# Building the first group's x parts in place, and k^T v head by head, in a one-core attention plus two-MLP kernel

## The chip, the cores and the metric

The kernel runs on one core of a Trainium2 chip. The metric is device time of one execution in microseconds (us), lower is better. The times of the kernel before are three executions; the profile is of a separate, fourth one.

## What is computed

Linear attention for 4 batches and 8 heads, 576 tokens of 64 features: per head `kv = k^T v` (64 x 64), `out = q kv`, then a root-mean-square norm of each token's 64 features with a gain. The heads are put side by side to 2304 tokens of 512 features, and two MLPs follow, each `x -> act(x w_in) w_out` with 2048 hidden features; the first act is softplus, the second a leaky ReLU of slope 0.01. All in float32:

```python
kv = einsum('bhsd,bhse->bhde', k, v);  out = einsum('bhsd,bhde->bhse', q, kv)
x = out / sqrt(mean(out * out) + 1e-06) * g_norm      # then heads side by side
x = softplus(x @ w_in) @ w_out                        # moe_
x = leaky_relu(x @ w_in, 0.01) @ w_out                # moe2_
```

The weights arrive as 64-bit floats; "decode" below makes float32 of them.

## The kernel before, in words

**Order of the work.** Every piece of work is registered with `op(cost, fn, reads, writes)`; `Plan.run` is a list scheduler that goes through all of them at build time with estimated costs (PE, A = ScalarE, D = VectorE, P = GpSimd, S = a DMA issued by SyncE, N = nothing) and due times, and so fixes the order of instructions on each engine. In the times it assumes, DMAs of kind S share one DMA resource; the reload of x parts that GpSimd issues (line 784) stands in it as 1.0 us of GpSimd time.

**Attention.** A unit is two heads of one batch, 16 units in all. `load(u)` brings q, k, v (five units ahead at most). `T(u)` copies q and k from the loaded order (partition, head, row, feature) to (partition, row, head, feature) in `qp` and `kp` (lines 337 to 341, on whichever engine the plan picks), transposes q on TensorE (lines 397, 401) and makes k^T v of both heads at once (lines 405, 408): four 128 x 128 matmuls and one over the 64 left-over tokens. The 128 x 128 result holds the two wanted 64 x 64 blocks on its diagonal; line 423 multiplies it by a block mask of ones and zeros into `kvm`. `O(u)` multiplies q by `kvm` (lines 436, 442), `normal` makes the norm, `X(u)` transposes the normed tokens into `xy` (features x tokens).

**MLPs.** Tokens are taken in 3 tiles of 768 (2 blocks of 384), hidden features in groups of 512 (4 groups for each MLP). In every group and tile there are two steps s, each with seven products of a Strassen-like scheme in float32r with hi and lo parts: `product(s, i)` (line 802, six matmuls) reads weights from `wst` and the x part `xe[i]`; `after` makes the activation; `quarter` multiplies by w_out (lines 900 and 916) one step later. The seven x parts of a tile are sums or differences of 384-token blocks of `xy`: `minus` (line 740) where a difference is needed, then `split_part`: a ScalarE copy to float32r (line 711) and a subtraction for the low part (line 706). There is one set of seven buffers `xe`, so a part of the next tile can go into `xe[i]` only after the second step's `product(s, i)` has read it.

**x parts in the first group of each MLP.** The first tile's parts are made in `xe` itself during attention. For tiles 1 and 2 the four parts that are differences (1, 2, 4, 6) are made one step ahead in a two-buffer stage `rc`, stored to the DRAM scratch `xscr` (line 758) and then brought into `xe[i]` by a GpSimd-issued DMA (line 784) once `xe[i]` is free; the three plain parts (0, 3, 5) are split straight from `xy` into `xe[i]`. In the later groups all parts come from `xscr`.

**Buffers.** `mf` (24 KiB for each partition) and `lf` (7 KiB, free only once attention's norm is done) hold among others two raw weight buffers `raw` (both in `mf`, used in turn by the weight chunks), the decoded weights `sraw`/`half`, and the activation inputs `cA` (one in `mf`, one in `lf`) and `cB`.

Of the kernel before, what the change touches and what calls it, by code (L numbers as in the profile page):

```python
# [8 lines left out]
F32 = mybir.dt.float32  # L9
F32R = mybir.dt.float32r  # L10
I32 = mybir.dt.int32
# [8 lines left out]
class Plan:  # L20
# [9 lines left out]
    DMA_ISSUE, DMA_START, DMA_DONE = 0.57, 1.1, 1.0  # L30

# [31 lines left out]
    def span(self, o):  # L63
        if "S" in o["cost"]:
            return self.DMA_ISSUE + self.DMA_START + o["cost"]["S"] + self.DMA_DONE
        return min(o["cost"].values())

    def run(self):
# [3 lines left out]
        free = {e: 0.0 for e in ("PE", "A", "D", "P", "S", "N")}  # L72
# [16 lines left out]
        while True:  # L89
            best = None  # L90
            for e, c in cand.items():
                if not c:
                    continue
                t = max(free[e], min(o["at"][e] for o in c))
# [16 lines left out]
            if e == "S":  # L111
                free[e] = t + self.DMA_ISSUE
# [16 lines left out]
def linear_attention_two_mlps(  # L129
# [36 lines left out]
    P = 128  # L166
# [37 lines left out]
    mask = const.tile([P, P], F32, name="mask")  # L204
    nc.vector.memset(mask, 0.0)
    nc.vector.memset(mask[0:D, 0:D], 1.0)
    nc.vector.memset(mask[D:P, D:P], 1.0)
# [13 lines left out]
    SIZE = {"ra": 70, "mf": 24, "rb": 54, "rc": 12, "lf": 7}  # L221
# [43 lines left out]
    raw = [Reg("mf", at * KI, [DM, 2], I32) for at in (0, 4)]  # L265

    SRAW = (("mf", 8), ("lf", 0))
# [11 lines left out]
    xt = [Reg("mf", at * KI, [2, BN]) for at in (12, 15)]  # L279
# [5 lines left out]
    cB = Reg("mf", 21 * KI, [2, BN])  # L285
    cA = [Reg("mf", 18 * KI, [2, BN]), Reg("lf", 4 * KI, [2, BN])]
# [15 lines left out]
    kp = ring(attp, "kp", 2, [P, 4, 2, D])  # L302
# [9 lines left out]
    fm = ring(mstp, "fm", 2, [P, 20])  # L312
    for t_ in ss:
        nc.vector.memset(t_, 1.0)
# [65 lines left out]
    def T(u):  # L380
# [3 lines left out]
        for nm, dst in (("q", qp), ("k", kp)):  # L384
            copy_to(
                dst[i], lda[nm][u % NLD].rearrange("p h r d -> p r h d"), 512,
                [(nm, u % NLD)], [(nm + "p", i)],
            )
        p0 = 2 * i if u < U_H else 0
        p1 = p0 + 1  # L390
        kv = ps[p1][:, 2 * P:3 * P]
# [11 lines left out]
        def f_kv(e):  # L403
            for r in range(4):
                nc.tensor.matmul(  # L405
                    kv, kp[i][:, r, :, :], va[:, :, r, :], start=(r == 0), stop=False
                )
            nc.tensor.matmul(kv, kl[:, h2, :], vl[:, h2, :], start=False, stop=True)  # L408

        for j in range(2):  # L410
# [6 lines left out]
            if j:  # L417
                op(
                    {"PE": 1.1}, f_kv,
                    [("kp", i), ("v", u % NLD), ("kr", b % 2), ("vr", b % 2)], [("ps", p1)],  # L420
                )
                op(
                    {"D": 0.22}, lambda e: nc.vector.tensor_tensor(kvm[i], kv, mask, ALU.mult),
                    [], [("ps", p1), ("kvm", i)],
                )
# [129 lines left out]
    def decode_w(F, which, a_reg):  # L555
        ph, f = F // NF, F % NF
        src = ((w1, w2), (w3, w4))[ph][which]
        ri = chunk_no[0] % 2
        chunk_no[0] += 1
        r_, t_ = raw[ri].ap, sqr  # L560
        low, high = r_[:, :, 0], r_[:, :, 1]

        def f_l(e):
            if which == 0:
# [4 lines left out]
            else:  # L569
# [4 lines left out]
        rk, tk, ak = raw[ri].keys(), [("sqr",)], a_reg.keys()  # L574
# [4 lines left out]
                a_reg.ap.bitcast(F32), high.bitcast(F32), AF.Copy, scale=2.0 ** -112  # L579
# [11 lines left out]
                t_, low, 29, t_, ALU.logical_shift_right, ALU.bitwise_or  # L591
# [175 lines left out]
    def x_load(tp, i, at_hand):  # L767
# [3 lines left out]
        if i in PLAIN:  # L771
# [11 lines left out]
            {"P": 1.0},  # L783
# [187 lines left out]
    for i in range(NU + XL):  # L971
# [19 lines left out]
       + [(t, i) for t in ("qp", "kp", "kvm") for i in range(2)]  # L991
# [15 lines left out]
    for s in range(2 * NT2 + 2):  # L1007
# [7 lines left out]
        for i in range(7):  # L1015
            if t < NT2:
                product(s, i)
                after(s, i)
                if t + 1 < NT2 and u == 0 and t + 1 in fresh:
                    x_part((t + 1) % NTP, i, xstage)  # L1020
                if t + 1 < NT2 and u == 1:
                    x_load((t + 1) % NTP, i, t + 1 in fresh)
# [59 lines left out]
```

## Time and profile before

| what | value |
|---|---|
| median of 3 runs | 856.74 us (854.68 to 857.86) |
| profiled execution's own time | 858.63 us |
| its span, first to last instruction | 856.9 us |
| TensorE busy | 830.3 us (97% of the span) |
| VectorE, ScalarE, GpSimd busy | 572.2, 449.5, 97.6 us |
| mean granted TensorE clock | 0.998 of full speed |
| moved by DMA | 172.73 MB |

Busy times of different engines overlap. What lies outside the span is 858.63 - 856.9 = 1.7 us.

### The profile page before, as it was taken

Reading aid. Unit: us, or ns where it says so; the run is one execution under the profiler, and the core shown is the slowest. Engines: PE = TensorE matmul, PEld = TensorE weight load, DVE = VectorE, ACT = ScalarE, POOL = GpSimd, SP = SyncE. Lnnn points to the kernel's source line nnn. Section 1 sums busy time; section 2 is a strip of 40 time slices with the busy share of each in tenths; the row PEclk is TensorE's granted clock in tenths of the full one; section 3 lists DMA queues with packets and bytes.
Section 4 is the critical chain, followed back from the end, with each engine's and each line's share of the span. In section 5 each row is a group of like instructions: output and inputs, shape, how many; then the busy total and the mean of one; then the engine's idle time right before and its main releaser. Section 6 shows DMA issues by size and latency. Waiting matters only on the chain.

```text
span 856.9 us, 11971 instructions
## 1 busy us (share of the span) xinstructions
PE 830.3 (97%) x4512; PEld 772.8 (90%) x4512; DVE 572.2 (67%) x911; ACT 449.5 (52%) x730; POOL 97.6 (11%) x152
## 2 busy tenths in 40 slices
PE   7998879999999999999999999999999999999997
PEld 5877769999999999999999998898988889898986
DVE  2779958786558673877778875766568855854332
ACT  1567847666445553645456665755455544553340
POOL 1476210000000000000000000000000000100000
PEclk9999999999999999999999999999999999999999
DMA  9984679667527646547757867645635852643613
GB/s 280 319 260 173 202 283 342 228 209 229 188 88 235 202 142 225 170 153 229 244 198 236 310 242 269 223 165 190 227 95 181 275 172 82 203 147 93 203 49 98
DMA packets 80024, 172.73 MB, mean 202 GB/s; under 512 B 11616, under 2 KB 54112, under 8 KB 79968
## 3 DMA queue, kind: packets, MB, share of 16 engines
q1 hardware_dynamic: 66720, 99.63, 35.0%
q0 software_dynamic: 13248, 72.36, 25.4%
q8 instruction: 35, 0.57, 0.3%
q14 instruction: 21, 0.17, 0.1%
HBM read 141.30 MB, written 30.67 MB: 201 GB/s over the span
## 4 chain that ended last, share of the span: by engine, by line
PE 88%; DMA 5%; DVE 4%; ACT 2%; issue 1%; POOL 0%; SPq 0%; POOLq 0%; DVEq 0%
PE ps L802 38%; PE ps L900 22%; PE ps L916 22%; PE ps L436 2%; DMA ra<-xscr 1%; DMA mf<-in_moe_w_in_dram 1%; PE ps L405 1%; DMA xscr<-rc 1%; PE ps L397 1%; PE ps L528 1%; DMA qa<-in_q_dram 1%; PE ps L442 1%; PE ps L408 1%; DVE xn L506 0%; DVE ra L659 0%
## 5 line engine op out<-in xcount | busy, mean ns | idle before, releaser
L802 PE MATMUL ps<-ra 128*128 128x384 f32 x2016 | 406.0, 336 | 10.0 <-DMA ra<-xscr 7.7
L802 PEld LDWEIGHTS ps<-ra 128*128 128x128 f32 x2016 | 357.4, 188 | 27.0 <-issue 6.5
L900 PE MATMUL ps<-rb 128*128 128x384 f32 x1152 | 227.1, 335 | 0.0
L916 PE MATMUL ps<-rb 128*128 128x512 f32 x864 | 225.0, 394 | 0.4 <-ACT xy L678 0.4
L900 PEld LDWEIGHTS ps<-rb 128*128 128x128 f32 x1152 | 202.6, 188 | 0.0
L916 PEld LDWEIGHTS ps<-rb 128*128 128x128 f32 x864 | 159.7, 188 | 24.7 <-ACT xy L678 1.1
L832 DVE TENSOR_TENSOR mf<-ps,mf 128x384 f32<-128x384 f32 x120 | 66.7, 557 | 156.5 <-PE ps L802 124.5
L784 POOL DMA_DIRECT2D ra<-xscr x92 | 49.2, 535 | 653.4 <-PE ps L802 605.5
L825 ACT ACTIVATE mf<-ps 128x384 f32<-128x384 f32 x120 | 58.7, 492 | 99.2 <-PE ps L802 98.5
L683 DVE TENSOR_TENSOR xy<-ps,xy 128x384 f32<-128x384 f32 (+1 forms) x126 | 77.4, 614 | 30.1 <-PE ps L916 20.8
L858 DVE TENSOR_TENSOR rb<-mf,rb 128x768 fp32r<-128x768 f32 x72 | 68.4, 951 | 1.9 <-ACT rb L853 1.8
L711 ACT ACTIVATE ra<-mf 128x768 fp32r<-128x768 f32 x58 | 48.7, 841 | 29.8 <-PE ps L802 28.6
L853 ACT ACTIVATE rb<-mf 128x768 fp32r<-128x768 f32 x72 | 61.0, 847 | 2.1
L706 DVE TENSOR_TENSOR ra<-mf,ra 128x768 fp32r<-128x768 f32 x55 | 53.5, 972 | 12.3 <-ACT ra L711 12.0
L845 ACT ACTIVATE mf<-mf 128x768 f32<-128x768 f32 (+1 forms) x36 | 26.6, 739 | 60.1 <-DVE mf L832 60.1
L839 ACT ACTIVATE mf<-mf 128x768 f32<-128x768 f32 (+1 forms) x36 | 26.5, 735 | 45.5 <-DVE mf L832 45.5
L590 DVE SCALAR_TENSOR_TENSOR sqr<-mf,sqr 128x512 int32<-128x512 int32 x64 | 46.9, 733 | 1.2
L578 ACT ACTIVATE mf<-mf 128x512 f32<-128x512 f32 x34 | 22.6, 666 | 27.4 <-DMA mf<-in_moe_w_in_dram 19.8
L678 ACT ACTIVATE xy<-ps 128x384 f32<-128x384 f32 (+1 forms) x33 | 17.4, 531 | 18.0 <-PE ps L900 14.7
L858 DVE TENSOR_TENSOR rb<-lf,rb 128x768 fp32r<-128x768 f32 x24 | 22.9, 954 | 3.7 <-ACT rb L853 3.7
L832 DVE TENSOR_TENSOR lf<-ps,lf 128x384 f32<-128x384 f32 x24 | 13.4, 558 | 16.9 <-PE ps L802 16.8
L596 DVE SCALAR_TENSOR_TENSOR mf<-mf,sqr 128x512 int32<-128x512 int32 x34 | 23.7, 698 | 0.4
(97 smaller groups left out, 646.5 us busy)
## 6 DMA issues: line engine op xcount, KB each, us to landing
ra<-xscr POOLq DMA_DIRECT2D x92, 768.0 KB, 6.0
mf<-xscr SPq DMA_DIRECT2D x54, 384.0 KB, 5.5
mf<-in_moe_w_in_dram SPq DMA_DIRECT2D x32, 512.0 KB, 4.4
mf<-in_moe_w_out_dram SPq DMA_DIRECT2D x32, 512.0 KB, 4.0
xscr<-rc SPq DMA_DIRECT2D x20, 768.0 KB, 4.0
xscr<-xy SPq DMA_DIRECT2D x18, 384.0 KB, 4.8
qa<-in_q_dram SPq DMA_DIRECT2D x16, 256.0 KB, 5.2
ka<-in_k_dram SPq DMA_DIRECT2D x16, 256.0 KB, 5.1
```

Source lines behind the costliest of these rows:

```text
L590: lambda e: nc.vector.scalar_tensor_tensor(t_, low, 29, t_, ALU.logical_shift_right, ALU.bitwise_or), rk + tk, tk,
L683: {"D": t_d(n)}, lambda e: nc.vector.tensor_tensor(dst, src, dst, ALU.add),
L706: ENG[e].tensor_tensor(e_[:, 1, :, :], src(), e_[:, 0, :, :].bitcast(F32), ALU.subtract)
L711: {"A": t_a(n)}, lambda e: nc.scalar.activation(e_[:, 0, :, :], src(), AF.Copy),
L784: lambda e: nc.gpsimd.dma_start(out=flat(xe[i]).ap, in_=xscr[7 * tp + i]),
L802: nc.tensor.matmul(o, w_[:, a, c:c + P], e_[:, b, kk, :], start=(not on and kk == 0 and n == 0), stop=(kk == 1 and n == 2), skip_group_che ...
L825: {"A": t_a(BN)}, lambda e: nc.scalar.activation(c[:, m, :], src, AF.Copy),
L832: lambda e: nc.vector.tensor_tensor(c[:, m, :], src, c[:, m, :], ALU.add),
L853: {"A": t_a(n)}, lambda e: nc.scalar.activation(g[:, 0, :, :], c.ap, AF.Copy),
L858: lambda e: nc.vector.tensor_tensor(g[:, 1, :, :], c.ap, g[:, 0, :, :].bitcast(F32), ALU.subtract),
L900: nc.tensor.matmul(y[:, :BN], w_[m][:, a, js], G_[:, b, m, :], start=(u == 0 and m == 0 and i == 0), stop=(u == 1 and m == 1 and i == 2),)
L916: nc.tensor.matmul(y, G_[:, a, m, js], w_[m][:, b, :], start=(u == 0 and m == 0 and i == 0), stop=(u == 1 and m == 1 and i == 2),)
```

## The change

It does five things. (1) For tiles 1 and 2 of the first MLP's first group, all seven x parts are made in `xe[i]` itself, in the second step, after `product(s, i)` has read the old part; the stage `rc` and the reload from DRAM are left out there, the store to `xscr` for the later groups stays, and the subtractions may also go to GpSimd. The first group of the second MLP keeps the stage. (2) k^T v is made head by head from `ka` as loaded: twice four matmuls with 128 x 64 weights and one over the left-over tokens, the second head into partitions 64 to 127; the copy `kp` is gone. (3) The mask is gone: `kvm` is zeroed once, and two copies of 64 x 64 a unit put the blocks in. (4) The second raw weight buffer moves to `lf`, so the first six weight chunks use one raw buffer; the second `cA` moves to `mf`; `mf` shrinks and `lf` grows by 1 KiB. (5) The plan has a new kind G, a DMA that GpSimd issues, with 2.25 us on the shared DMA resource; the reload of line 784 is now of that kind.

```diff
-        if "S" in o["cost"]:
-            return self.DMA_ISSUE + self.DMA_START + o["cost"]["S"] + self.DMA_DONE
+        if self.DMA_BY.keys() & o["cost"].keys():
+            return self.DMA_ISSUE + self.DMA_START + sum(o["cost"].values()) + self.DMA_DONE
...
-    SIZE = {"ra": 70, "mf": 24, "rb": 54, "rc": 12, "lf": 7}
+    SIZE = {"ra": 70, "mf": 23, "rb": 54, "rc": 12, "lf": 8}
...
-    raw = [Reg("mf", at * KI, [DM, 2], I32) for at in (0, 4)]
+    raw = [Reg(n, at * KI, [DM, 2], I32) for n, at in (("mf", 0), ("lf", 4))]
...
-    cA = [Reg("mf", 18 * KI, [2, BN]), Reg("lf", 4 * KI, [2, BN])]
+    cA = [Reg("mf", at * KI, [2, BN]) for at in (17, 4)]
...
-        for nm, dst in (("q", qp), ("k", kp)):
+        for nm, dst in (("q", qp),):
...
-        kv = ps[p1][:, 2 * P:3 * P]
+        kv = ps[p1][:, 2 * P:2 * P + D]
+        ka = lda["k"][u % NLD]
...
         def f_kv(e):
-            for r in range(4):
+            for h in range(2):
+                o = kv[h * D:(h + 1) * D, :]
+                for r in range(4):
+                    nc.tensor.matmul(
+                        o, ka[:, h, r, :], va[:, h, r, :], start=(r == 0), stop=False
+                    )
                 nc.tensor.matmul(
-                    kv, kp[i][:, r, :, :], va[:, :, r, :], start=(r == 0), stop=False
-                )
-            nc.tensor.matmul(kv, kl[:, h2, :], vl[:, h2, :], start=False, stop=True)
+                    o, kl[:, 2 * hp + h, :], vl[:, 2 * hp + h, :], start=False, stop=True
+                )
...
-                op(
-                    {"D": 0.22}, lambda e: nc.vector.tensor_tensor(kvm[i], kv, mask, ALU.mult),
-                    [], [("ps", p1), ("kvm", i)],
-                )
+                def f_m(e):
+                    for h in range(2):
+                        hs = slice(h * D, (h + 1) * D)
+                        nc.vector.tensor_copy(kvm[i][hs, hs], kv[hs, :])
+
+                op({"D": 0.3}, f_m, [], [("ps", p1), ("kvm", i)])
...
-        ri = chunk_no[0] % 2
+        ri = chunk_no[0] % 2 if chunk_no[0] >= 6 else 0
...
         op(
-            {"P": 1.0},
+            {"G": 2.25},
             lambda e: nc.gpsimd.dma_start(out=flat(xe[i]).ap, in_=xscr[7 * tp + i]),
...
-                if t + 1 < NT2 and u == 0 and t + 1 in fresh:
-                    x_part((t + 1) % NTP, i, xstage)
-                if t + 1 < NT2 and u == 1:
+                straight = t + 1 <= 2
+                if t + 1 in fresh and (not straight and u == 0 or straight and u == 1):
+                    x_part((t + 1) % NTP, i, () if straight else xstage)
+                elif t + 1 < NT2 and u == 1:
                     x_load((t + 1) % NTP, i, t + 1 in fresh)
```

## Rows read from the trace of the kernel before

**Rows 1.** Busy time by stretch: length, each engine (instructions), clock, DMA share, GB/s.
```profile
20.50:57.00 36.50, 36.19 (x251) 29.35 (x251) 27.08 (x61) 21.93 (x47) 19.35 (x28) 1.00 1.04 323
57.00:93.00 36.00, 31.69 (x215) 26.06 (x213) 34.22 (x62) 26.83 (x56) 23.54 (x23) 1.00 0.49 173
93.00:113.00 20.00, 15.16 (x75) 13.53 (x75) 18.87 (x25) 15.83 (x26) 4.83 (x4) 0.91 0.71 251
113.00:124.00 11.00, 7.59 (x42) 7.33 (x43) 2.31 (x4) 2.13 (x4) 1.09 (x2) 1.00 0.87 318
124.00:155.00 31.00, 29.36 (x168) 28.75 (x167) 24.34 (x37) 20.55 (x37) 2.11 (x4) 1.00 0.84 302
155.00:490.00 335.00, 335.00 (x1935) 334.96 (x1934) 241.83 (x382) 185.63 (x290) 22.70 (x43) 1.00 0.61 202
490.00:850.00 360.00, 359.28 (x1776) 320.88 (x1774) 216.73 (x324) 173.08 (x269) 22.08 (x41) 1.00 0.53 174
```

**Rows 2.** What TensorE waited for in the whole span: total us, times, longest.
```profile
PE ps L802 <- DMA ra<-xscr: 7.7, 4, 2.4
...
PE ps L802 <- ACT lf L825: 1.4, 1, 1.4
```

**Rows 3.** Chain of work, 100 to 126 us: start us, us, what.
```profile
106.29 9.87 DMA xscr<-rc
...
116.70 5.54 DMA ra<-xscr
...
123.69 1.05 PE ps L900 x6
124.73 1.04 PE ps L802 x6
```

**Rows 4.** TensorE's timeline, 94 to 128 us: start us, us, instruction, idle before.
```profile
94.28 1.34 PE L802 MATMUL ps<-ra 128*128 128x384 f32 x6
...
109.31 2.13 PE L802 MATMUL ps<-ra 128*128 128x384 f32 x6 [2.44 <-DMA ra<-xscr]
111.24 1.16 PE L900 MATMUL ps<-rb 128*128 128x384 f32 x3
...
126.65 1.20 PE L802 MATMUL ps<-ra 128*128 128x384 f32 x6
```

**Rows 5.** Groups of instructions up to 130 us, by form: count, busy us, mean ns.
```profile
L341 POOL TENSOR_SCALAR kp<-ka 128x512 f32<-128x512 f32 x9 | 5.9, 656 | 7.6 <-issue 2.9 <-PE ps L405 2.6 <-DMA ka<-in_k_dram 2.1
...
L711 ACT ACTIVATE rc<-mf 128x768 fp32r<-128x768 f32 x6 | 5.0, 834 | 0.0
L706 DVE TENSOR_TENSOR rc<-mf,rc 128x768 fp32r<-128x768 f32 x5 | 4.8, 952 | 0.7 <-ACT rc L711 0.7
...
L423 DVE TENSOR_TENSOR kvm<-ps,mask 128x128 f32<-128x128 f32 x16 | 4.6, 286 | 10.8 <-PE ps L408 10.5 <-PE ps L442 0.3
...
L355 DVE COPY qt<-ps 128x256 f32<-128x256 f32 x7 | 2.9, 415 | 0.0
```

**Rows 6.** Chain of work in attention, all on TensorE: start us, us, what.
```profile
9.16 2.00 PE ps L405 x8
...
45.37 0.26 PE ps L540 x2
...
47.11 0.36 PE ps L442 x2
...
50.08 0.20 PE ps L401
...
51.09 0.89 PE ps L405 x8
51.98 0.41 PE ps L408 x2
```

**Rows 7.** DMA issues on the page: count, KB each, median us to landing.
```profile
mf<-in_moe_w_out_dram SPq DMA_DIRECT2D x32, 512.0 KB, 4.0
```

**Rows 8.** TensorE's instructions of line 405 from 20.5 to 57 us, by form.
```profile
L405 PE MATMUL ps<-va,kp 128*128 128x128 f32 x72 | 9.9, 281 | 0.0
```

More of the change, by code (lines that the diff above doesn't have):

```diff
@@ L30 @@
     DMA_ISSUE, DMA_START, DMA_DONE = 0.57, 1.1, 1.0
+    DMA_BY = {"S": "S", "G": "P"}
     def __init__(self):
@@ L71, in run @@
                 o["due"] = min(o["due"], s["due"] - self.LAT - self.span(o))
-        free = {e: 0.0 for e in ("PE", "A", "D", "P", "S", "N")}
+        free = {e: 0.0 for e in ("PE", "A", "D", "P", "S", "G", "N")}
         dma = 0.0
@@ L93, in run @@
                     continue
-                t = max(free[e], min(o["at"][e] for o in c))
+                t = max(free[self.DMA_BY.get(e, e)], min(o["at"][e] for o in c))
                 o = min(
@@ L110, in run @@
             o["eng"], o["start"] = e, t
-            if e == "S":
-                free[e] = t + self.DMA_ISSUE
+            if e in self.DMA_BY:
+                free[self.DMA_BY[e]] = t + self.DMA_ISSUE
                 dma = max(dma, t + self.DMA_ISSUE + self.DMA_START) + o["cost"][e]
@@ L203, in linear_attention_two_mlps @@
     make_identity(nc, ident)
[L204 to L207, printed above, removed]
     graw = const.tile([P, 1], F32, name="graw")
@@ L264, in linear_attention_two_mlps @@
     sqr = const.tile([P, DM], I32, name="sqr")
-    raw = [Reg("mf", at * KI, [DM, 2], I32) for at in (0, 4)]
-    SRAW = (("mf", 8), ("lf", 0))
+    raw = [Reg(n, at * KI, [DM, 2], I32) for n, at in (("mf", 0), ("lf", 4))]
+    SRAW = (("mf", 7), ("lf", 0))
     sraw = [Reg(n, at * KI, [4, 256]) for n, at in SRAW]
@@ L278, in linear_attention_two_mlps @@
     xe = [Reg("ra", 6 * i * KI, [2, 2, BN]) for i in range(7)]
-    xt = [Reg("mf", at * KI, [2, BN]) for at in (12, 15)]
+    xt = [Reg("mf", at * KI, [2, BN]) for at in (11, 14)]
     xstage = [Reg("rc", at * KI, [2, 2, BN]) for at in (0, 6)]
@@ L284, in linear_attention_two_mlps @@
     gA = [Reg("rb", (12 + 6 * i) * KI, [2, 2, BN]) for i in range(3)]
-    cB = Reg("mf", 21 * KI, [2, BN])
-    cA = [Reg("mf", 18 * KI, [2, BN]), Reg("lf", 4 * KI, [2, BN])]
+    cB = Reg("mf", 20 * KI, [2, BN])
+    cA = [Reg("mf", at * KI, [2, BN]) for at in (17, 4)]
     dram = ctx.enter_context(tc.tile_pool(name="dram", bufs=1, space=bass.MemoryType.DRAM))
@@ L301, in linear_attention_two_mlps @@
     qp = ring(attp, "qp", 2, [P, 4, 2, D])
-    kp = ring(attp, "kp", 2, [P, 4, 2, D])
     qt = ring(attp, "qt", 2, [P, S])
@@ L312, in linear_attention_two_mlps @@
     fm = ring(mstp, "fm", 2, [P, 20])
+    for t_ in kvm:
+        nc.vector.memset(t_, 0.0)
     for t_ in ss:
@@ L419, in T @@
                     {"PE": 1.1}, f_kv,
-                    [("kp", i), ("v", u % NLD), ("kr", b % 2), ("vr", b % 2)], [("ps", p1)],
+                    [("k", u % NLD), ("v", u % NLD), ("kr", b % 2), ("vr", b % 2)], [("ps", p1)],
                 )
-                op(
-                    {"D": 0.22}, lambda e: nc.vector.tensor_tensor(kvm[i], kv, mask, ALU.mult),
-                    [], [("ps", p1), ("kvm", i)],
-                )
+                def f_m(e):
[3 more added lines that the diff above has]
+                op({"D": 0.3}, f_m, [], [("ps", p1), ("kvm", i)])
             from_psum(qt[i][:, c0:c0 + n], ps[p0 + j][:, :n], n, p0 + j, [("qt", i, j)])
@@ L557, in decode_w @@
         src = ((w1, w2), (w3, w4))[ph][which]
-        ri = chunk_no[0] % 2
+        ri = chunk_no[0] % 2 if chunk_no[0] >= 6 else 0
         chunk_no[0] += 1
-        r_, t_ = raw[ri].ap, sqr
-        low, high = r_[:, :, 0], r_[:, :, 1]
+        r, t_ = raw[ri], sqr
         def f_l(e):
+            r_ = r.ap
             if which == 0:
@@ L572, in f_l @@
                 )
-        rk, tk, ak = raw[ri].keys(), [("sqr",)], a_reg.keys()
+        rk, tk, ak = r.keys(), [("sqr",)], a_reg.keys()
         op({"S": 1.46}, f_l, (), rk)
@@ L578, in decode_w @@
             lambda e: nc.scalar.activation(
-                a_reg.ap.bitcast(F32), high.bitcast(F32), AF.Copy, scale=2.0 ** -112
+                a_reg.ap.bitcast(F32), r[:, :, 1].bitcast(F32), AF.Copy, scale=2.0 ** -112
             ), rk, ak,
@@ L590, in decode_w @@
             lambda e: nc.vector.scalar_tensor_tensor(
-                t_, low, 29, t_, ALU.logical_shift_right, ALU.bitwise_or
+                t_, r[:, :, 0], 29, t_, ALU.logical_shift_right, ALU.bitwise_or
             ), rk + tk, tk,
@@ L990, in linear_attention_two_mlps @@
     op({"N": 0.0}, attention_done, (), granules("rb")
-       + [(t, i) for t in ("qp", "kp", "kvm") for i in range(2)]
+       + [(t, i) for t in ("qp", "kvm") for i in range(2)]
        + [("qt", i, j) for i in range(2) for j in range(2)]
```

## Prediction

> **What bounds the kernel now.** I first read busy time by stretch. From 155 us TensorE is never short of work: 335.00 of 335 us, then 359.28 of 360 [rows 1]. The change leaves the matmuls there as they are, so it can only win or lose before 155 us, where there are four different stretches. From 20.5 to 57 us TensorE is the bound (36.19 of 36.5 us busy) and VectorE has 9.4 us to spare. From 57 to 93 us VectorE is the bound (34.22 of 36), TensorE idle for 4.3 us. From 93 to 113 us VectorE is still nearly full (18.87 of 20), TensorE idle for 4.84 us. From 113 to 124 us both idle, TensorE 3.41 and VectorE 8.69 us, while the DMA engines are 87% busy; from 124 to 155 TensorE idles for 1.64 us more [rows 1]. Then the waits: `product` (line 802) waited 7.7 us in four waits for x parts coming back from DRAM, and once 1.4 us for ScalarE [rows 2]. The chain says what made them late: the store of a staged part took 9.87 us, its reload 5.54 us [rows 3]. The timeline shows a second price: after the 2.44 us wait, six matmuls take 1.93 us (109.31 to 111.24) instead of the 1.04 us of a warm six [rows 3, 4], in a stretch whose mean granted clock is 0.91 [rows 1].
>
> **The x parts in place: what it can give.** TensorE's idle time from 93 to 155 us is 4.84 + 3.41 + 1.64 = 9.9 us [rows 1]. The slow clock adds 1.93 - 1.04 = 0.9 us for the six matmuls at 109.31 and, for the three at 111.24 (1.16 us of pipelined duration; warm six start to start take 1.05, so three about 0.52), about 0.6 us [rows 3, 4]. Together 11.4 us; this is the ceiling.
>
> What remains of it? In place there is no DMA between product(1, i) and product(2, i), but a chain: ScalarE copy 0.83 us, VectorE subtraction 0.95 us [rows 5], both allowed only once TensorE has read the old part. Seven parts need 7 x 0.83 = 5.8 us of ScalarE and, with four differences of the same length, 11 x 0.95 = 10.5 us of VectorE. That work isn't new: 93 to 113 us holds most of it already, for the stage. VectorE was through its backlog at 113 us. On TensorE, from 94.28 us on, the second step's seven products and the next step's seven are 14 x 1.04 = 14.6 us, and between them lie 16 groups of three w_out matmuls at 0.52 = 8.4 us [rows 3, 4]: 23 us of work, to 117.3 us if nothing stalls, where the last product of these now starts at 126.65 and ends near 127.7 us [rows 4]. Since parts are due one after another and the w_out groups can be put between, a finish of the parts at 108 to 113 us (VectorE's backlog, less what GpSimd takes) fits with little waiting. I allow 2 us of new waits and 1 us of the old ones at the end of attention (table load, last norm), so the gain is 11.4 - 3 = 8.4 us. Bounds: 11 us with no wait, 3 us if VectorE and ScalarE become the gate (rival 2). For tile 2 the parts have a whole step of 15 us and more, with VectorE at 24.34 of 31 us [rows 1], so I charge nothing; if that cover is gone, it costs the 1.64 us counted above.
>
> **k^T v head by head: what it costs.** All rows here are warm and on the chain. Eight matmul records with 128 columns take 0.89 us, 0.111 each; a unit's two with 64 rows take 0.41 us [rows 6], so 0.41 - 2 x 0.111 = 0.19 us goes with the change of the array's shape. Two with 64-wide weights take 0.36 us: 0.14 us for that change. One transpose of 64 columns takes 0.20, two 0.26: 0.06 us for one more record of 64 columns [rows 6]. A unit is now 0.89 + 0.41 = 1.30 us of TensorE. After, it has 20 records of 64 columns and four changes of shape (into 128 x 64, into 64 x 64, for each head): 20 x 0.06 + 2 x (0.14 + 0.19) = 1.86 us, so +0.56 us. The way back to full size is paid in both versions. Bounds: if a 64-column record is no shorter than a 128-column one, 20 x 0.111 + 0.66 = 2.88 us, +1.6 us a unit; if the changes between the heads' halves cost nothing and records follow at half of 0.111, 1.1 us, -0.2 us a unit. I take the middle, since the two transposes are the only records with 64 moving columns.
>
> A rule of the Trainium skill speaks for the upper bound: "TensorE: Matmul & The Clock Gate", Part 3, says that a weight load overlaps running matmuls only where its row group differs, and here all loads of a head have one row group. By it each record pays its load as well as its stream, which gives the upper bound's order of cost. The trace doesn't bear it out for the 128-wide case: loads with one row group lie between the eight records that follow each other every 0.111 us [rows 6].
>
> Where does +0.56 us fall? Nine units run in the TensorE-bound stretch (72 records of line 405 in it, eight a unit [rows 8]): 5.0 us. Two run before, in the first 20 us, where the same eight take 2.00 us instead of 0.89 [rows 6]; at twice the cost they add 2.2 us. The last five run where VectorE is the bound and TensorE's 4.3 us idle covers their 2.8 us; without the cover they are a loss. So TensorE leaves its stretch 7.2 us later. Not all of this reaches 93 us: VectorE, the bound after it, gets 7 us more of spare time ahead of its own stretch and can do part of its backlog (decode, x parts of tile 0) there. I take half, 3.6 us; bounds 0 and 7.2, and for the upper price of a record (9 x 1.6 + 2 x 3.2 = 20.8 us) some 10 to 21 us.
>
> **The rest.** The 16 copies to `kp` vanish; nine were GpSimd's (5.9 us, 0.66 each), which was no bound [rows 1, 5]. A pair of 64 x 64 copies takes the place of a 0.286 us multiplication. By the nearest copy out of PSUM, 0.415 us for 256 columns [rows 5], a pair costs between 0.2 and 0.5 us: -1.4 to +3.4 us of VectorE in 16 units, partly before its bound stretch. Together with the `kp` copies that other engines lose I take 0. The single raw buffer puts chunk loads of 4.0 us [rows 7] one after another; the third and fifth chunk wait for their target buffers anyway, and the weights of the second step are needed only at 94.28 us [rows 4], which hides it; one load bare on VectorE's backlog would cost up to 4 us. The seventh and eighth chunk: the eighth now waits for `lf`, free near 93 us, but its weights multiply only after some 110 us; hidden. Stores of the parts move one step later on SyncE's queue, which waits in order: a store waiting for its subtraction holds the weight loads of the next group behind it, and these have until 155 us. The removed reloads are 8 of 128 x 1536 x 4 bytes, about 6 MB in a stretch where DMA was 71 to 87% busy [rows 1], so the other transfers come sooner. The new kind G changes the order in the plan; after 155 us TensorE is full whatever it is, so 0, with 1 us either way before.
>
> **The sum**, against the profiled execution's 858.63 us: -8.4 + 3.6 = -4.8, 853.8 us. That execution is 1.9 us above the median, so the median of runs goes from 856.74 to about 851.9 us.
>
> **Rivals.** (1) The upper price of a 64-column record: TensorE gives up 20.8 us before 57 us, of which some 12 us arrive; 856.7 - 8.4 + 12 = 860.3 us. For it: the weight loads, as many as the matmuls, must hide behind streams half as long. Against: one more 64-column transpose costs 0.06 us. It ends slower than before from 8.4 us of delay at 93 us on. (2) The wait moves from the DMA to ScalarE and VectorE: the copies of the parts queue behind softplus and activation copies, the parts are ready at VectorE's pace some 5 us later than I say, and new waits eat 5 of the 8.4 us: 856.7 - 3.4 + 3.6 = 856.9 us, no change. For it: VectorE at 18.87 of 20 us; against: it idled 8.69 of the following 11 us [rows 1]. (3) The matmuls of the two heads cost no more than before (lower bound), so nothing arrives: 856.7 - 8.4 - 0.5 = 847.8 us.
>
> **How the numbers follow.** What measurement can tell from no change is 0.5%, 4.3 us: under 852.4 faster, over 861.0 slower. Forecast 45% (own range 847 to 856), rival 1 17%, rival 2 20%, rival 3 18%. Faster: a little over half of the forecast's cases (0.26), rival 3 (0.18), a few of rival 2 (0.03): 0.47. Slower: about half of rival 1, 0.09, and 0.03 from bare loads or a bad order: 0.12. The rest, 0.41, is within 0.5%. Range 843 to 863 us: it holds the forecast, rivals 2 and 3 and most of rival 1.
>
> **What would show it.** Right: no wait of `product` for a DMA before 155 us, the clock at 1.00 there, the last product of the third step near 120 us; two-head k^T v of 1.9 us a unit; TensorE full but later up to some 64 us. Wrong: waits of line 802 for lines 706 or 711 above 4 us in all (rival 2), records with 64 columns 0.1 us apart (rival 1), or TensorE short of work after 155 us, for which I have no term.

## The result, and the profile after

The changed kernel takes 864.42 us in the median of four runs (863.28 to 867.42); the kernel before took 857.25 us beside it (854.68 to 857.86). The ratio is 1.0085 with an interval of 1.006 to 1.011: slower by some 7 us, where 5 us faster was forecast. The profiled execution took 864.63 us with a span of 862.6 us, against a span of 856.9 us before.

Busy time by stretch from 57 us on, after, with the columns of [rows 1]:

```profile
57.00:93.00 36.00, 33.65 (x263) 27.17 (x263) 31.61 (x58) 23.88 (x48) 24.04 (x23) 1.00 0.42 152
93.00:113.00 20.00, 18.24 (x98) 17.25 (x96) 18.06 (x29) 15.63 (x26) 11.78 (x7) 0.91 0.70 243
113.00:124.00 11.00, 6.41 (x26) 6.41 (x27) 10.30 (x9) 6.14 (x12) 6.66 (x4) 0.69 0.31 120
124.00:155.00 31.00, 24.10 (x128) 23.78 (x127) 29.06 (x30) 17.65 (x30) 17.61 (x9) 0.89 0.59 194
155.00:490.00 335.00, 335.00 (x1934) 335.00 (x1933) 236.67 (x372) 180.86 (x280) 22.47 (x42) 1.00 0.59 196
490.00:850.00 360.00, 360.00 (x1792) 323.49 (x1791) 223.49 (x336) 177.55 (x274) 22.70 (x42) 1.00 0.55 179
```

After 155 us nothing has changed: TensorE is full. From 93 to 155 us it idles 1.76 + 4.59 + 6.90 = 13.3 us, against 9.9 before [rows 1]. VectorE, which had 2.31 of 11 us to do from 113 to 124 us, now has 10.30, and 29.06 of the next 31. GpSimd is busy for 36.1 us of the three stretches, against 8.0 before.

What TensorE waited for, from 93 us on:

```profile
PE ps L807 <- DVE mf L837: 6.9, 1, 6.9
PE ps L807 <- ACT mf L830: 4.7, 1, 4.7
```

`product` (now line 807) no longer waits for a DMA, where it did for 7.7 us [rows 2]. It waits longer for two things that have nothing to do with the x parts: ScalarE's copy of a product out of PSUM (830) and VectorE's addition on one (837). TensorE's timeline shows what each wait costs besides:

```profile
117.59 2.29 PE L807 MATMUL ps<-ra 128*128 128x384 f32 x6 [4.70 <-ACT mf L830]
119.68 1.16 PE L905 MATMUL ps<-rb 128*128 128x384 f32 x3
120.64 1.69 PE L807 MATMUL ps<-ra 128*128 128x384 f32 x6
122.17 1.20 PE L905 MATMUL ps<-rb 128*128 128x384 f32 x6
...
147.95 2.29 PE L807 MATMUL ps<-ra 128*128 128x384 f32 x6 [6.90 <-DVE mf L837]
150.04 2.12 PE L905 MATMUL ps<-rb 128*128 128x384 f32 x6
151.96 1.43 PE L807 MATMUL ps<-ra 128*128 128x384 f32 x6
153.23 1.21 PE L905 MATMUL ps<-rb 128*128 128x384 f32 x6
```

Start to start, six matmuls after each of these two idle times take 2.09 us instead of the 1.04 of a warm six, at a granted clock of 0.50 (117.6 to 119.6 us and 148 to 150 us): the 1.2 GHz level. Over the three groups after the first wait and the three after the second, the loss against 1.04 us for six (0.52 for three) is 1.05 + 0.44 + 0.49 and 1.05 + 0.88 + 0.23, in all 4.1 us, against 1.5 us before. Idle and slow clock together were 11.4 us, which I meant to bring to 3; they are 17.4 us. A third slow stretch lies ahead of these two, after waits of 1.21 and 0.44 us among attention's last transposes: 24 matmuls of `product` from 97.54 to 103.36 us take 5.82 us, at a granted clock of 0.53 up to 101 us, where the kernel before had 4.45 us for them (97.06 to 101.51). With these 1.4 us the sum is 18.8 us.

The chain of waits leads from TensorE to VectorE:

```profile
114.40 2.57 DVE rb L863
117.05 0.50 ACT mf L830
117.59 2.30 PE ps L807 x6
...
146.83 0.60 DVE rb L623
147.43 0.48 DVE mf L837
```

A subtraction on VectorE (863, a part of an activation) that took 0.95 us before takes 2.57 us; the ScalarE copy may overwrite its input only then, and the product waits for the bank that this copy empties. Ahead of the second wait, five VectorE instructions between 131.5 and 143.7 us take 2.07 to 2.59 us each, instead of 0.43 to 0.95, and the addition (837) stands behind them. The engines' timelines beside each other, GpSimd first:

```profile
106.80 2.01 POOL L745 TENSOR_TENSOR mf<-xy 128x768 f32<-128x768 f32 x1
108.76 2.30 POOL L711 TENSOR_TENSOR ra<-xy,ra 128x768 fp32r<-128x768 f32 x1
...
113.89 2.25 POOL L711 TENSOR_TENSOR ra<-xy,ra 128x768 fp32r<-128x768 f32 x1
...
122.32 2.44 POOL L745 TENSOR_TENSOR mf<-xy 128x768 f32<-128x768 f32 x1
```

and VectorE:

```profile
107.48 1.88 DVE L595 SCALAR_TENSOR_TENSOR sqr<-mf,sqr 128x512 int32<-128x512 int32 x1
109.39 2.22 DVE L601 SCALAR_TENSOR_TENSOR lf<-lf,sqr 128x512 int32<-128x512 int32 x1
...
114.40 2.56 DVE L863 TENSOR_TENSOR rb<-mf,rb 128x768 fp32r<-128x768 f32 x1
...
122.97 0.54 DVE L837 TENSOR_TENSOR mf<-ps,mf 128x384 f32<-128x384 f32 x1
```

Read the ends, not the starts. GpSimd's instructions end at 108.81, 111.06 and 116.14 us; the three VectorE instructions that began meanwhile end at 109.36, 111.61 and 116.96: 0.55, 0.55 and 0.82 us later, each 0.13 or 0.14 us less than its own length (0.69, 0.69 and 0.95 us when nothing runs on GpSimd). They stood still while GpSimd worked. The fourth, which takes one operand from PSUM, ran at its usual 0.54 us inside a GpSimd instruction. So did all nine of line 837 that ran beside one up to 155 us (0.54 to 0.56 us), and the eleven of line 511, another with a PSUM operand (0.67 to 0.69 us). The Trainium skill states this in "SBUF — State Buffer", section "Who interferes with whom": the two engines share a pair of ports under an exclusive lock, and a VectorE instruction with two SBUF inputs contends with a GpSimd instruction that reads SBUF. These ends agree with it.

How much of it there is, by groups and forms from 93 to 155 us, after:

```profile
L711 POOL TENSOR_TENSOR ra<-mf,ra 128x768 fp32r<-128x768 f32 x6 | 12.0, 1999 | 17.0 <-ACT ra L716 16.9
L863 DVE TENSOR_TENSOR rb<-mf,rb 128x768 fp32r<-128x768 f32 x7 | 11.5, 1649 | 0.3 <-ACT rb L858 0.3
L711 POOL TENSOR_TENSOR ra<-xy,ra 128x768 fp32r<-128x768 f32 x5 | 10.2, 2040 | 7.7 <-ACT ra L716 7.7
L595 DVE SCALAR_TENSOR_TENSOR sqr<-mf,sqr 128x512 int32<-128x512 int32 x5 | 7.7, 1538 | 0.1
L745 POOL TENSOR_TENSOR mf<-xy 128x768 f32<-128x768 f32 x3 | 6.9, 2302 | 0.2
L601 DVE SCALAR_TENSOR_TENSOR lf<-lf,sqr 128x512 int32<-128x512 int32 x4 | 6.8, 1696 | 0.1
...
L745 POOL TENSOR_TENSOR mf<-xy,mf 128x768 f32<-128x768 f32 x2 | 4.3, 2154 | 0.2
```

The same stretch in the kernel before, where line 858 is now 863, 590 is 595 and 596 is 601:

```profile
L858 DVE TENSOR_TENSOR rb<-mf,rb 128x768 fp32r<-128x768 f32 x6 | 5.7, 954 | 1.2 <-ACT rb L853 1.2
...
L590 DVE SCALAR_TENSOR_TENSOR sqr<-mf,sqr 128x512 int32<-128x512 int32 x6 | 5.2, 865 | 0.0
...
L596 DVE SCALAR_TENSOR_TENSOR lf<-lf,sqr 128x512 int32<-128x512 int32 x4 | 2.7, 684 | 0.0
```

GpSimd took 6 + 5 + 3 + 2 = 16 subtractions of the x parts, which would be 16 x 0.95 = 15.2 us of VectorE. The three VectorE groups shown took 7 x (1.649 - 0.95) + 5 x (1.538 - 0.69) + 4 x (1.696 - 0.69) = 13.2 us longer for it, and GpSimd needs 2.0 us for what VectorE does in 0.95. The standing still of these three groups alone all but eats the help; others grew too (those of line 589, 0.43 us alone, to 1.12 and 0.72 us on average), and e1 below shows VectorE busier with the help than without it.

In attention the chain has the new products of two heads, 39.42 to 41.15 us:

```profile
39.42 0.61 PE ps L406 x8
40.03 0.25 PE ps L409 x2
40.28 0.61 PE ps L406 x8
40.89 0.26 PE ps L409 x2
```

A unit takes 1.73 us, against 1.30 [rows 6]. The 1.30 us are not every unit's, though: where the unit followed matmuls of another array shape, as at 21.02 us on the chain of the kernel before, it took 1.09 + 0.41 = 1.50 us. Over the last 14 units the traces have 1.71 us on average after and 1.36 us before. The last transposes of attention start at 97.13 us, where they started at 93.48 us before.

### The profile page after: what moved, and what is told of

The parts are those of the page before. It is cut to its first block, busy times and chain, and to the rows that moved or that the text cites. A ratio compares the mean times of both kernels' runs of the same rounds, so it can differ in the third digit from the quotient of the medians.

```text
span 862.6 us, 12264 instructions
## 1 busy us (share of the span) xinstructions
PE 835.9 (97%) x4672; PEld 779.8 (90%) x4672; DVE 585.4 (68%) x914; ACT 444.7 (52%) x714; POOL 120.9 (14%) x157
## 4 chain that ended last, share of the span: by engine, by line
PE 91%; DVE 6%; issue 2%; ACT 1%; DMA 1%; SPq 0%; POOL 0%; DVEq 0%; ACTq 0%; POOLq 0%
PE ps L807 39%; PE ps L921 23%; PE ps L905 22%; PE ps L406 2%; PE ps L441 2%; DVE sqr L595 1%; DVE sqr L589 1%; PE ps L409 1%; PE ps L396 1%; PE ps L533 1%; DVE rb L863 1%; DMA va<-in_v_dram 1%; DVE mf L837 1%; PE ps L447 0%; DVE mf L601 0%
## 5 line engine op out<-in xcount | busy, mean ns | idle before, releaser
L807 PE MATMUL ps<-ra 128*128 128x384 f32 x2016 | 409.1, 338 | 11.6 <-DVE mf L837 6.9
L837 DVE TENSOR_TENSOR mf<-ps,mf 128x384 f32<-128x384 f32 x144 | 80.0, 557 | 176.6 <-PE ps L807 144.0
L830 ACT ACTIVATE mf<-ps 128x384 f32<-128x384 f32 x144 | 70.7, 492 | 116.3 <-PE ps L807 113.2
L863 DVE TENSOR_TENSOR rb<-mf,rb 128x768 fp32r<-128x768 f32 x96 | 96.2, 1002 | 4.6 <-ACT rb L858 4.5
L858 ACT ACTIVATE rb<-mf 128x768 fp32r<-128x768 f32 x96 | 81.4, 848 | 2.7
L716 ACT ACTIVATE ra<-mf 128x768 fp32r<-128x768 f32 x66 | 55.5, 841 | 30.5 <-PE ps L807 29.5
L850 ACT ACTIVATE mf<-mf 128x768 f32<-128x768 f32 (+1 forms) x48 | 32.8, 684 | 61.3 <-DVE mf L837 61.3
L844 ACT ACTIVATE mf<-mf 128x768 f32<-128x768 f32 (+1 forms) x48 | 32.6, 680 | 55.6 <-DVE mf L837 55.5
L595 DVE SCALAR_TENSOR_TENSOR sqr<-mf,sqr 128x512 int32<-128x512 int32 x35 | 30.9, 883 | 0.9
L601 DVE SCALAR_TENSOR_TENSOR lf<-lf,sqr 128x512 int32<-128x512 int32 x30 | 24.6, 821 | 0.4
L406 PE MATMUL ps<-va,ka 128*64 128x64 f32 x256 | 23.3, 239 | 1.0 <-DMA va<-in_v_dram 1.0
L406 PEld LDWEIGHTS ps<-va,ka 128*64 128x64 f32 x256 | 19.0, 148 | 4.2 <-issue 2.2
```

Of the source, the lines that this page charges most:

```text
L406: nc.tensor.matmul(o, ka[:, h, r, :], va[:, h, r, :], start=(r == 0), stop=False)
L601: lambda e: nc.vector.scalar_tensor_tensor(a_reg.ap, a_reg.ap, -(1 << 31), t_, ALU.bitwise_and, ALU.bitwise_or), tk + ak, ak,
L716: {"A": t_a(n)}, lambda e: nc.scalar.activation(e_[:, 0, :, :], src(), AF.Copy),
L807: nc.tensor.matmul(o, w_[:, a, c:c + P], e_[:, b, kk, :], start=(not on and kk == 0 and n == 0), stop=(kk == 1 and n == 2), skip_group_che ...
L830: {"A": t_a(BN)}, lambda e: nc.scalar.activation(c[:, m, :], src, AF.Copy),
L837: lambda e: nc.vector.tensor_tensor(c[:, m, :], src, c[:, m, :], ALU.add),
```

## The experiments

There were two theories at the start. One: the x parts of the first group, once in place, may go to GpSimd (the program allows it only where there is no stage), and GpSimd stops VectorE. Its rival: the loss is the price of k^T v on TensorE. Later runs had theories of their own, which their expectations name. Each kernel was timed beside the kernel before; kernels of different rows are compared by their ratios to it, times 857 us.

| kernel | us, median | ratio to before | interval |
|---|---|---|---|
| e1: after, those parts on VectorE only | 851.41 | 0.9940 | 0.9919 to 0.9961 |
| e2: after with the old k^T v | 859.22 | 1.0011 | 0.9992 to 1.0030 |
| e3: before with the new k^T v alone | 868.59 | 1.0131 | 1.0102 to 1.0160 |
| e4: before, GpSimd allowed for those parts | 861.72 | 1.0048 | 1.0025 to 1.0071 |
| e5: e1 with the old k^T v | 855.56 | 0.9973 | 0.9958 to 0.9989 |
| e6: e1, k^T v in another order | 845.43 | 0.9853 | 0.9828 to 0.9879 |
| e8: e1, reload at its old cost in the plan | 854.44 | 0.9943 | 0.9919 to 0.9967 |
| e9: e5, no subtraction on GpSimd | 851.29 | 0.9920 | 0.9894 to 0.9946 |
| e10: e6, no subtraction on GpSimd | 850.01 | 0.9925 | 0.9902 to 0.9948 |
| e11: e6, `split_w2` on VectorE only | 845.04 | 0.9860 | 0.9830 to 0.9890 |
| e14: before, no subtraction on GpSimd | 862.81 | 1.0074 | 1.0051 to 1.0096 |
| e15: after, k^T v in the order of e6 | 858.94 | 1.0015 | 0.9993 to 1.0036 |
| e16: e3, k^T v in the order of e6 | 856.14 | 0.9972 | 0.9954 to 0.9990 |

**e1: the parts stay in place, but only VectorE may subtract.**

```diff
-    def x_part(tp, i, stages=()):
+    def x_part(tp, i, stages=(), pool=True):
-                split_part(xe[i], src, sk, True)
+                split_part(xe[i], src, sk, pool)
-            op(either(2 * BN, not stages), fn, ...)
+            op(either(2 * BN, pool and not stages), fn, ...)
-                x_part(..., () if straight else xstage)
+                x_part(..., () if straight else xstage, False)
```

> The changed kernel, but the x parts of tiles 1 and 2 of the first group may not go to GpSimd: differences and subtractions are VectorE's alone. Theory L (a VectorE instruction whose operands all lie in SBUF waits for the GpSimd instruction that runs beside it): from 93 to 155 us the subtractions of line 863 and the decode steps go back from 1.5 to 1.7 us on average to 0.95 and 0.69 us, the two waits of TensorE (4.7 and 6.9 us) shrink to under 3 us in all, and the time falls by 8 to 11 us, to 853 to 857 us. Rival C (making the parts in place is too late, whichever engine subtracts, because the parts queue behind the activation work): VectorE gets some 15 subtractions of 0.95 us more, 14 us in that stretch, the waits stay above 10 us and the time at 864 us or more.

It is 12.4 us faster than the changed kernel (0.994 against 1.0085), more than the 8 to 11 us expected, and 5 us faster than before. Busy time by stretch and the waits of TensorE from 93 to 155 us:

```profile
93.00:113.00 20.00, 17.51 (x104) 16.10 (x103) 18.20 (x32) 17.56 (x30) 5.18 (x3) 1.00 0.52 172
113.00:124.00 11.00, 8.42 (x41) 8.10 (x40) 8.30 (x9) 3.87 (x8) 6.96 (x2) 0.84 0.62 249
124.00:155.00 31.00, 31.00 (x181) 31.00 (x180) 25.20 (x39) 23.26 (x41) 0.00 (x0) 1.00 0.52 182
```

```profile
PE ps L905 <- POOL rb L623: 2.6, 1, 2.6
PE ps L807 <- ACT mf L844: 1.3, 1, 1.3
```

The two long waits are gone and TensorE idles 5.1 us instead of 13.3. VectorE, which now does all of those subtractions itself, is busy for 51.7 us of the 62, less than the 57.4 us with GpSimd's help; its subtractions of line 863 take 0.95 us again:

```profile
L863 DVE TENSOR_TENSOR rb<-mf,rb 128x768 fp32r<-128x768 f32 x7 | 6.7, 951 | 1.1 <-ACT rb L858 1.1
```

The mean granted clock of its executions is 0.999 in the median, against 0.990. The plan also orders the work otherwise when GpSimd may not take these parts, so the 12.4 us are the price of the whole permission; how much of it is the standing still alone was not measured. A wait of 2.6 us is left, for a subtraction that GpSimd still does (`split_w2`, line 623).

**e4, the counterpart: the stage stays, and GpSimd is allowed for the same parts.**

```diff
-            op(either(2 * BN, not stages), fn, ...)
+            op(either(2 * BN, pool or not stages), fn, ...)
-            split_part(e_, src, sk, not stages)
+            split_part(e_, src, sk, pool or not stages)
...
-            split_part(xe[i], *x_block(tp, *PLAIN[i]))
+            split_part(xe[i], *x_block(tp, *PLAIN[i]), pool)
...
```

> The kernel before, stage and reload kept, but the differences and subtractions for tiles 1 and 2 of the first group may go to GpSimd. Theory L: VectorE's instructions beside them take 1.5 us and more where they took 0.95 and 0.69, the staged parts are stored no earlier, TensorE's idle time from 93 to 155 us grows from 9.9 to 13 us or more, and the time is 859 to 864 us. Rival C: GpSimd only helps, or does nothing, as the reload from DRAM sets the pace: 854 to 857.5 us.

It costs 0.48%, 4 us, a third of what it costs in place. From 93 to 155 us VectorE is lengthened as in the changed kernel, in fewer groups (first fence). `product` still waits for its reloads, and now for VectorE too (second, of the whole span). TensorE idles 11.5 us from 93 to 155 us, not the 13 us that had been expected:

```profile
L858 DVE TENSOR_TENSOR rb<-mf,rb 128x768 fp32r<-128x768 f32 x6 | 7.3, 1218 | 0.0
...
L596 DVE SCALAR_TENSOR_TENSOR mf<-mf,sqr 128x512 int32<-128x512 int32 x4 | 4.1, 1034 | 0.0
```

```profile
PE ps L802 <- DMA ra<-xscr: 8.3, 4, 3.9
...
PE ps L802 <- DVE mf L832: 3.8, 3, 1.7
```

So GpSimd's help harms either way, and with the parts in place, where VectorE has little to spare, it costs three times as much. That the place of the parts and not only the order of the plan makes the difference is argued, not shown.

**e2 and e3: the two halves of the change apart.** e2 puts the old k^T v back into the changed kernel; e3 is its counterpart, the new k^T v in the kernel before:

```diff
-                nc.tensor.matmul(kv, kp[i][:, r, :, :], va[:, :, r, :], ...)
+            for h in range(2):
+                for r in range(4):
+                    nc.tensor.matmul(kv[h * D:(h + 1) * D, :], ka[:, h, r, :], va[:, h, r, :], ...)
```

> The changed kernel with k^T v as before: copy of k, both heads in one matmul, mask. What attention lost (the last transpose of attention starts 3.7 us later in the changed kernel) is undone. Theory A (the delay of TensorE passes on to the end): the time falls by 3 to 4 us, to 860.5 to 861.5 us, and the last transposes of attention start near 93.5 us. Rival B (the later stalls absorb it, since VectorE is the bound there): less than 1 us, 863.5 to 864.5 us.

> The kernel before with only k^T v head by head, without copy and mask; stage, reload and buffers as before. Theory A: a unit's k^T v takes 1.74 us of TensorE instead of 1.30, the end of attention comes 3 to 4 us later and the time is 860 to 861 us. Rival B (VectorE's spare time takes the delay up, or the wait for the reload does): 857 us, as before.

Undone in the changed kernel, the new k^T v gives back 6.3 us; alone, in e3, it costs 1.31%, 11.2 us. TensorE's own surplus would be 16 x 0.43 = 6.9 us by the unit of [rows 6]; by the averages above it is 14 x 0.35 us and 0.4 us in the first two units, about 5 us. In e3 the waits for the reloads stay (next line, of the whole span, against 7.7 us in [rows 2]), and the granted clock is 0.73 from 113 to 124 us, where the kernel before had 1.00 [rows 1]:

```profile
PE ps L806 <- DMA ra<-xscr: 8.6, 3, 3.1
```

```profile
113.00:124.00 11.00, 5.54 (x23) 4.78 (x23) 8.17 (x11) 4.49 (x8) 2.44 (x2) 0.73 1.00 363
```

So neither 11.2 nor 6.3 us is the price of k^T v alone. In e3 the clock has a part: its mean is 0.990 in the median of e3's executions, 0.994 in those of the kernel before beside them; if the time goes with the clock, that is some 3 us of 857. In e2 TensorE idles 7.3 us from 93 to 155 us, where the changed kernel idled 13.3.

**e6, e15 and e16: the same products with fewer changes of the array's shape.** The eight matmuls over 128 tokens of both heads come first, then the two over the left-over tokens; count, operands and the plan's costs and dependencies stay:

```diff
             for h in range(2):
                 for r in range(4):
                     nc.tensor.matmul(kv[h * D:(h + 1) * D, :], ka[:, h, r, :], ...)
-                nc.tensor.matmul(o, kl[:, 2 * hp + h, :], ...)
+            for h in range(2):
+                nc.tensor.matmul(kv[h * D:(h + 1) * D, :], kl[:, 2 * hp + h, :], ...)
```

> Parts in place by VectorE alone, k^T v from k as loaded, but in another order: the eight matmuls over 128 tokens of both heads, then the two over the left-over tokens, so that the array changes its shape twice in a unit and not four times. If a change of shape costs 0.15 us, as the price of head by head was worked out, a unit's k^T v falls from 1.74 to 1.4 to 1.45 us, 16 units by 5 us, and the time from 851.4 to 847 to 849 us. If the price lies in the number of matmuls (the load of weights), the unit stays at 1.7 us and the time at 850.5 to 852 us.

> The changed kernel with GpSimd as it is there, only k^T v in the order with two changes of shape. If the two are independent: 864.4 less the same 6 us that the order gave with VectorE alone (851.4 to 845.4), 857 to 860 us, no better than the kernel before: GpSimd's share is the larger. If the shorter attention alone were the cure: 850 us or less.

> The kernel before with k^T v from k as loaded, no copy, no mask, as in the run that changed k^T v alone (868.6 us), but in the order with two changes of shape: on TensorE a unit then costs 1.16 us, less than before (1.30 us). Stage and reload stay. Theory P (the 11 us lost by k^T v alone are TensorE's time for head by head): the loss turns into a gain, 852 to 857 us. Theory R (most of it is the other order of the work that the plan makes once the copy is gone, and what it does to the reload and to the clock): it falls by the same 6 us as twice before, to 861 to 864 us, and stays above the kernel before.

The chain of e6 in attention has a unit at 0.90 + 0.26 = 1.16 us, less than either value of the old form, 1.30 and 1.50 us:

```profile
39.59 0.90 PE ps L405 x16
40.49 0.26 PE ps L410 x4
```

That is 0.57 us a unit and 9.1 us in all off TensorE, nearly twice what the expectation had, which put a unit with two changes of shape less at 1.4 to 1.45 us. The starts of the single records show the rest. In the changed kernel the eight of one head start 0.058 us apart (39.457, 39.515, 39.574 us and so on), and the second head's come after them. In e6 two such series of eight run beside each other: the first starts at 39.524 us and goes on to 39.982 us, the second starts at 39.813 us already. The two heads write different halves of the output's partitions (0 to 63 and 64 to 127); that this is what lets them overlap is argued, not shown. The time fell by 7.5 us in e6 against e1, 6.0 us in e15 against the changed kernel, and 13.6 us in e16 against e3. So k^T v is on the path whichever way the parts are made, and e3's surplus goes away with TensorE's: before e16 it could as well have been the missing copy and the mask, which the plan orders otherwise. In e16 the clock has a part again: 13.6 us are more than TensorE saved, and its mean clock is 0.994 in the median, against 0.990 in e3. With this order alone (e15), the changed kernel is level with the kernel before.

**e5 and e9, and what they left open.** e5 is e1 with the old k^T v; e9 is e5 with `either` giving VectorE alone everywhere.

> Parts in place, their differences and subtractions for tiles 1 and 2 by VectorE alone, and k^T v as before (both heads at once, copy and mask). Theory A (the price of head by head, 0.43 us of TensorE in each of 16 units, 7 us, arrives almost whole): 4 to 7 us less than with head by head and VectorE alone (851.4 us), so 845 to 848 us, faster than both kernels. Rival B (attention's delay is taken up by the later stalls once these are small): 850 to 852 us.

> Parts in place and k^T v as before, and no subtraction at all on GpSimd, in attention neither (first tile's x parts, the splits of the first weights). Theory L (each GpSimd subtraction of some 2 us holds up a VectorE instruction with operands in SBUF for about as long as it saves, and the other way round): no worse than the version with GpSimd in attention, 0 to 4 us faster than it. Rival (GpSimd is real help where VectorE is the bound, 57 to 93 us, as 13 or more subtractions of 0.95 us move to VectorE): 4 us slower or more than it.

By e2, e5 should have been faster than e1; it is 2.8 us slower (0.9973 against 0.9940). With the copy `kp` back, the plan puts attention in another order, and the surplus of TensorE is not all that differs between the two: over the whole span TensorE waits 10.8 us for VectorE's copies `qp` and norms `xn` in e5, and 7.2 us in e1. Up to 93 us it idles 12.1 us against 8.3, which eats most of what the old form saves. e9 is 4.5 us faster than e5, so GpSimd's subtractions have a part in it; how large, and in which waits, stays open. The cleanest measures of what k^T v's time on TensorE is worth are therefore e6, e15 and e16, each against its counterpart, where the plan has the same input; they measure the order, not the step from the old form to the new.

**e8: the plan's new cost of a reload.**

```diff
-            {"G": 2.25},
+            {"P": 1.0},
```

> Parts in place by VectorE alone, head by head, but the planner's price of the GpSimd-issued reload as it was before (1.0 us of GpSimd time, not a DMA of 2.25 us). If the price matters only for the order within the first 155 us: 850 to 853 us, the same as with the new price (851.4 us). If the new price reorders the long stretch too: TensorE short of work after 155 us in one of the two, and 2 us or more of difference.

No difference to e1 (0.9943 against 0.9940), as my zero for this part had it.

**e10, e14 and e11: should GpSimd subtract at all?** e10 and e14 let only VectorE subtract, in e6 and in the kernel before; e11 takes only `split_w2` from GpSimd.

```diff
-        return {"D": t_d(n), "P": t_p(n)} if beside else {"D": t_d(n)}
+        return {"D": t_d(n)}
```

> Parts in place, k^T v from k as loaded in the order with two changes of shape, and no subtraction on GpSimd at all. Theory L: the subtractions that GpSimd still makes in attention (19 up to 150 us, 34 us of its time) are no gain either; with the older k^T v the same step gave 4.3 us (855.6 to 851.3). Expected 841 to 845.5 us. Rival (VectorE is the bound between 57 and 93 us, and with the shorter k^T v it feels each of the 0.95 us subtractions): 846 us or more.

> The kernel before with no subtraction on GpSimd at all: stage, reload, k^T v of both heads, mask as they were. Theory L: the lock costs the kernel before too (19 GpSimd subtractions, 31 us), so 852 to 856 us. Rival (GpSimd's help is worth its price as long as there are few of them and they lie in attention): 858 us or more. The waits for the reload from DRAM, 7.7 us, stay in both.

> Parts in place by VectorE, the order with two changes of shape, and only the splits of the first w_out weights (line 625, which took 6.9 us once on GpSimd and held TensorE for 2.6 us) go to VectorE as well; the rest of attention may use GpSimd. If that one wait was real, 845.4 less 1.5 to 3 us: 842.5 to 844 us. If another wait takes its place: 845 to 846.5 us.

e10 loses 6.2 us to e6, and e14 loses 0.74%, 6.3 us, to the kernel before: on balance GpSimd's subtractions pay in these two, against theory L, while the same step from e5 to e9, with the old k^T v and the parts in place, gained 4.5 us. So what GpSimd's subtractions in attention are worth hangs on the rest of the kernel. In e10 the loss begins ahead of 93 us:

```profile
57.00:93.00 36.00, 26.39 (x198) 21.60 (x197) 28.50 (x54) 22.93 (x46) 6.45 (x15) 0.86 0.33 123
```

TensorE is busy there for 26.39 us at a clock of 0.86, where e6 had 31.87 us at 0.95. In e14 the loss appears after attention, where TensorE waits 4.0 and 3.6 us for reloads of parts:

```profile
113.00:124.00 11.00, 3.49 (x14) 2.69 (x13) 5.14 (x8) 3.35 (x6) 1.05 (x2) 0.67 0.88 320
```

Up to 155 us TensorE idles only 2.3 us more in e14 than in the kernel before; its mean clock is 0.991 in the median against 0.996, some 4 us of 857 by the same estimate.

e11 removed the 2.6 us wait for `split_w2` (line 625 in e6) and gained nothing (0.9860 against 0.9853): TensorE idles 2.4 us less from 93 to 113 us, but 1.6 us more before that. e6 is the fastest version together with e11, 1.5% ahead of the kernel before.

## Why the prediction was wrong, point by point

**The failed step** is the finish of the parts: "a finish of the parts at 108 to 113 us (VectorE's backlog, less what GpSimd takes) fits with little waiting", and with it "For tile 2 ... I charge nothing". I subtracted from VectorE what GpSimd would take, as if the two ran beside each other for nothing. In this stretch VectorE's work is subtractions and decoding with SBUF operands, and GpSimd's subtractions of 2 us each stopped it. VectorE was still at 10.30 of 11 us in the stretch where I had it idle, the gain of 8.4 us became a loss of 6.0 (11.4 to 17.4 us of idle and slow clock), and tile 2, charged at nothing, had the longer wait (6.90 us). With GpSimd kept off those parts the time is 851.41 us. My figure was 851.9, but the agreement is largely luck: e1 has a GpSimd wait of 2.6 us that I did not have, and a cheaper k^T v than I had. Nor do the two terms of my sum add up as I added them. The parts in place by VectorE alone (with the buffers and the plan's cost, which come along) gain 2.3 us with the old k^T v (e5 against the kernel before), 10.2 us with the order of e6 (e6 against e16), and 16.4 us with the new k^T v as changed (e1 against e3); I had 8.4 us for all of them.

The trace before held the warning: one group of decode instructions (590) averaged 0.976 us up to 93 us and 0.865 us from 93 to 155 us, against 0.684 for its kin of line 596 in the latter stretch. The long ones, 2.18 us at 63.43 us and 1.77 us at 108.86 us, each ended 0.55 us after a GpSimd subtraction beside it. I read means and did not ask what ran on GpSimd during the long ones.

**Rival 2** ("the wait moves from the DMA to ScalarE and VectorE") names the engines that came, 11.6 us of waits of `product` for them, but not by its mechanism, which was the queue of copies behind softplus, nor at its size, 5 us. Its sign, waits of line 802 for lines 706 or 711, did not come: what was late was not the parts but the activation's copies and additions behind stopped instructions.

**The DMA waits** went away before 155 us, as forecast, and 8 of the 92 reloads of that form did too. The clock "at 1.00 there" was wrong: 0.91, 0.69 and 0.89 in the three stretches, lowest after the two long waits.

**k^T v** had the right mechanism and sign. A unit rose by 0.43 us instead of 0.56, and by 0.35 on average, as my 1.30 us for the old one were those of the cheaper of its two kinds. The prices within were near: records of one head follow each other every 0.058 us (I had 0.06), which leaves 0.61 - 8 x 0.058 = 0.15 us for the change into 128 x 64 (0.14) and 0.25 - 2 x 0.058 = 0.13 us for the change into 64 x 64 (0.19). A unit with two changes less would so take some 1.45 us; that the two heads' records then also run beside each other, which takes off 0.3 us more, I had not thought of. The last transposes were 3.65 us later, near the 3.6 that I let pass; but TensorE idled 2 us less than before from 57 to 93 us [rows 1], and when k^T v alone was changed or reordered the time moved by 6.0 to 13.6 us the way that TensorE's time did, except between e1 and e5. "I take half" was too little: of 9.1 us saved on TensorE, 6.0 us (e15) and 7.5 us (e6) arrive, two thirds and more, and in e16 13.6 us, with the clock.

**Rival 1** falls: records of 64 columns follow each other every 0.058 us, those of 128 columns every 0.111 us. The rule of the Trainium skill that was weighed there ("TensorE: Matmul & The Clock Gate", Part 3) would have loads of one row group pay in full; the eight records of one head, 0.058 us apart with a load for each, don't show it. **Rival 3** falls too for the change as made, though e6 shows its price, below the old one, to be had by order alone.

**The rest at zero** holds as far as tested: e8 for the plan's cost, and TensorE full after 155 us. A pair of 64 x 64 copies takes 2 x 0.221 = 0.44 us by its group, inside the 0.2 to 0.5 that I gave; its share of the whole was not timed by itself, and neither were the single raw buffer and the moved `cA`.

## What to carry to other kernels

Work given to GpSimd is not free for VectorE: look at what VectorE runs there, and count the GpSimd instruction's whole length against it where its operands are in SBUF, and little where they come from PSUM. When a change removes a condition (here: the stage), ask which other choices hung on it; here the permission for GpSimd came along with the place. Matmuls of one array shape belong together; here those of the two heads then also ran beside each other: the order of twenty small ones was worth 6 us and more. And look at the clock beside the waits: some of these runs lost as much to it as to idle time.

## What the hardware showed beyond that

The hold works both ways. In e1, with VectorE full, a GpSimd subtraction of line 623 that takes 1.3 to 2.0 us elsewhere took 6.90 us, as its chain shows, and held TensorE for 2.6 us:

```profile
111.12 6.90 POOL rb L623
```

VectorE had no idle time beside it, and GpSimd came through only when VectorE ran an instruction with a PSUM operand (837, at 116.81 us): it ended 1.2 us after that one's start. The same subtraction ended 1.2 us after the start of the same addition in e5 (117.23 us) and in e6 (109.15 us), where it took 5.7 and 6.9 us.

An instruction with a single SBUF input and a constant was stopped as well: line 589 took 1.60 us at 123.44 us beside GpSimd's instruction of 122.32 to 124.76, against 0.43 alone. And a helper can pay in one stretch and harm in the next: the same permission was worth 6 us to the kernel before in attention (e14), and cost 12.4 us in the x parts (e1). In the kernel before, instructions with a PSUM operand and reductions, whose times stay the same beside GpSimd, make up 19.0 of the 37.7 us that VectorE's instructions sum to from 57 to 93 us, and 7.2 of 50.0 us from 93 to 155 us. That would explain it; it was not tried by itself, and e9 gained without GpSimd in attention.
